# Loading q of two groups together in 1 KB pieces, and moving some loads and casts, in a chunked attention that feeds a squared-ReLU FFN

## The chip, the cores and the metric

The program runs on one core of one Trainium2 chip. The metric is the device time of one execution in microseconds (us); lower is better. A run's time is that of the whole execution; the span of a profile goes from its first to its last instruction and is a little shorter.

## The reference, cut to what matters

```
q, k, v: [8 batches, 8 heads, 576 tokens, 64] f32     # attention only inside chunks of 64 tokens
scores = q_c @ k_c^T / 8 ; attn = softmax(scores) ; a = attn @ v_c
x = a.transpose(0, 2, 1, 3).reshape(4608, 512)
h = relu(x @ w_in)          # w_in [512, 2048]
out = (h * h) @ w_out       # w_out [2048, 512], out f32
```

## The kernel before, in words

The 4608 tokens are cut into 18 **groups** of 256 tokens (four chunks of 64), and two groups make a **block** of 512 tokens; there are nine blocks, 0 to 8. Groups 0 to 13, 16 and 17 are "whole": their four chunks lie one after the other in one batch, and the two groups of a block are neighbours. Groups 14 and 15 (block 7) gather the ninth chunk of each batch.

A block's work is written in 32 to 46 **slots**: first the slots of its first matmul (`ffn_in`, or `ffn_in_unit` from block 2 on, which saves products by sums and differences; lines 607 and 494), then those of its second (`ffn_out`, line 664, seven products `n`, `m`, `n`, `m`, `n`, `m`, `n` that take 14 slots in the same way). A `yield` ends a slot. Between slots the loop at the end of the file (lines 873 to 958) inserts, by the table `plan`, the attention work of the **next** block and the casts and transposes of the block **after next**, and, in the slots listed in `go_slots`, one piece of the loads of the block after next. What is left of the loads is issued at the end of the block. All this fixes only the order of instructions on each engine. Each engine then runs its own list in that order and waits at semaphores. All loads, the DMA transposes and most stores are issued by SyncE (SP), so in one order.

The steps of a group `g`:

- `qk_pieces(g)` loads q and k in f32 (lines 106 and 120). For q, partition p of the tile holds two neighbouring tokens of all eight heads: 512 bytes lie together in HBM. For k (from group 4 on) a piece of 256 bytes is one token of one head. `v_pieces(g)` loads v for even and odd heads (lines 148 and 152), nine pieces for the two groups of a block, in 256-byte pieces.
- C (`cast_q`, `cast_k`; CQ and CK apart) turns them to bf16 in one tile `qkb`, on GpSimd for groups below 8, on ScalarE from 8 on (lines 334 and 341). For q it sorts by "plane": first all even tokens, then all odd ones.
- TD is the DMA transpose of `qkb` to `qkT` (line 352), from group 4 on; earlier groups are transposed by TensorE.
- SC (`scores`, line 375) multiplies a group's 32 pairs of 64x64 tiles into PSUM and takes the exponential on ScalarE (line 386), which also puts the planes' columns back in order of token.
- AV (`values`, line 403) multiplies by v and normalizes on VectorE (lines 410 and 411), giving `x`.
- XT transposes `x` to `xT`, which the next block's first matmul reads: by TensorE up to group 5, by DMA (line 424) from group 6 on.

In `ffn_out`, ScalarE copies the first `n` product out of PSUM (line 728), and the third product's running sum again (line 737); the fifth product adds into the same bank and so waits for that second copy. At the fixed slots of blocks 3 to 8 the casts of the block after next stand on ScalarE's list around these copies.

A few lines that the steps rest on:

```python
            elif j in UNITS:
                go_slots = range(35)
                if far and is_whole(far[0]):
                    go_slots = [*range(6), *range(13, 17), *range(23, 35)]
                slots.update({SC: (4, 4), AV: (8, 13), XT: (12, 17)})
                if j == 3 or not is_whole(nxt[0] if nxt else 0):
                    slots.update({SC: (8, 8), AV: (11, 16), XT: (14, 19)})
```

Here j is the running block, and each pair has the slots for the two groups of the next block. In block 2 the pairs are SC (8, 10), AV (12, 16), XT (15, 19), and the casts and TD of groups 8 and 9 have slots 23 to 28. In all blocks with a unit, slots 0 to 18 are the first matmul, slots 19 to 32 the second.

Of the kernel before, what the change touches and what calls it, by code (L numbers as in the profile page):

```python
# [17 lines left out]
def kernel(  # L18
# [9 lines left out]
    nc = tc.nc  # L28

    B, H, S, D = q.shape  # L30
# [13 lines left out]
    CH = GT // 4  # L44
# [3 lines left out]
    chunks = whole[:-2] + rest + whole[-2:]  # L48

    def is_whole(g):  # L50
        return chunks[g][0][0] == chunks[g][3][0]

    FIRST_DMA_T = 4
    FIRST_DMA_X = 6
    SQUARES_ON_ACT = (10, 14, 3)
# [44 lines left out]
    def qk_pieces(g):  # L100
        q_sb = in_pool.tile([128, 2, H, D], FP32, name="q_sb")
        k_sb = in_pool.tile([128, 2, H, D], FP32, name="k_sb")
        qk[g] = (q_sb, k_sb)

        def pairs(dst, src, p, m, b, s):
            return lambda: nc.sync.dma_start(
                out=dst.rearrange("p t h d -> p (t h d)")[p:p + m // 2, :].rearrange(
                    "p (h e) -> p h e", h=H),
                in_=src[b, :, s:s + m, :].rearrange("h (s i) d -> s h (i d)", i=2))

        if is_whole(g):
            yield pairs(q_sb, q, 0, GT, *chunks[g][0])
        else:
            for c in range(4):
                yield pairs(q_sb, q, c * CH // 2, CH, *chunks[g][c])
        if g < FIRST_DMA_T:
            yield pairs(k_sb, k, 0, GT, *chunks[g][0])
            return
        for t, p, m, b, s in runs(g):
            yield lambda t=t, p=p, m=m, b=b, s=s: nc.sync.dma_start(  # L120
                out=k_sb[p:p + m, t, :, :],
                in_=k[b, :, s:s + m, :].rearrange("h s d -> s h d"))
# [58 lines left out]
    state = {}  # L181
# [148 lines left out]
    def cast_q(g):  # L330
        qkb = att_pool.tile([128, 2, 2 * H * D], BF16, name="qkb", bufs=2)
        state["qkb", g] = qkb
        copy = nc.gpsimd.tensor_copy if g < 8 else nc.scalar.copy
        copy(
            out=qkb[:, 0].rearrange("p (i h d) -> p i h d", i=2, h=H),
            in_=qk[g][0].rearrange("p t h d -> p (t h d)").rearrange(
                "p (h i d) -> p i h d", h=H, i=2))

    def cast_k(g):
        copy = nc.gpsimd.tensor_copy if g < 8 else nc.scalar.copy  # L340
# [13 lines left out]
            in_=qkb.rearrange("p w c -> p (w c)"))  # L354

    def scores(g):
        qkT = state.pop(("qkT", g))
        by_plane = g >= FIRST_DMA_T

        def queries(a, t, hp, p):  # L360
            x = qkT[64 * a:64 * a + 64, 0]
            if by_plane:
                p0 = (2 * t + p) * CH // 2
                return x[:, :, hp, p0:p0 + CH // 2]
            return x[:, t, hp, p * 64:p * 64 + 64]

        ps = ps_att.tile([128, 1024], FP32, name="ps_att")
        for hp in range(n_hp):
            for t in range(2):
                for a in range(2):  # L370
                    for p in range(2):
                        c = p ^ a
                        cols = slice(p * 64, p * 64 + 64)
                        o0 = a * 512 + hp * 128 + t * 64
                        nc.tensor.matmul(  # L375
                            out=ps[64 * c:64 * c + 64, o0:o0 + 64],
                            lhsT=qkT[64 * a:64 * a + 64, 1, t, hp, cols],
                            rhs=queries(a, t, hp, p),
                            start=True, stop=True)
        e = att_pool.tile([128, 2, n_hp, 2, 64], BF16, name="e")  # L380
        state["e", g] = e
        e_out, s_in = e.rearrange("p a h t q -> p (a h t q)"), ps
        if by_plane:
            e_out = e.rearrange("p a h t (q i) -> p (a h t) q i", i=2)
            s_in = ps.rearrange("p (b i q) -> p b q i", i=2, q=CH // 2)
        nc.scalar.activation(out=e_out, in_=s_in, func=AF.Exp, scale=scale)  # L386

    def values(g, tiles=(0, 1)):
# [484 lines left out]
    for j, grps in enumerate(blocks):  # L873
        nxt = blocks[j + 1] if j + 1 < len(blocks) else []
        far = blocks[j + 2] if j + 2 < len(blocks) else []
        plan = {}

        def at(slot, f, g):
            plan.setdefault(slot, []).append((f, g))

        if j == 0:
            loads, go_slots = pieces(far), range(17)
            at(28, sum_quarters(b11_p_b21, b11, b21), None)
            for slot, f in ((24, TA), (27, SC), (29, AV), (31, XT)):
                at(slot, f, nxt[0])
            at(31, TQ, nxt[1])
            at(31, TK, nxt[1])
            at(31, sum_quarters(b11_m_b22, b11, b22, ALU.subtract), None)
            phases = [first_ffn_in, ffn_out_by_ft(0)]
        elif j == 1:  # L890
            loads, go_slots = itertools.chain(*map(qk_pieces, far)), range(26, 48)
            for slot, f in ((4, SC), (8, AV), (12, XT)):
                at(slot, f, grps[1])
            for i, g in enumerate(nxt):
                for slot, f in ((16 + 4 * i, C), (21 + 4 * i, TD), (36 + i, SC), (38 + 2 * i, AV),
                                (41 + 2 * i, XT)):
                    at(slot, f, g)
            for i, g in enumerate(far):
                at(36 + 4 * i, C, g)
                at(42 + 3 * i, TD, g)  # L900
            at(2, sum_quarters(b11_p_b12, b11, b12), None)
            at(12, sum_quarters(b12_p_b22, b12, b22), None)
            at(20, sum_quarters(b21_p_b22, b21, b22), None)
            phases = [ffn_in(1, [(0, 256, FT_ORDER), (256, 256, FT_ORDER)]), ffn_out(1)]
        else:
            loads, go_slots = pieces(far), range(32)
            slots = {SC: (4, 4), AV: (7, 11), XT: (10, 14), C: (18, 22), TD: (20, 24)}
            if j == 3:
                slots.update({SC: (8, 8), AV: (10, 14), XT: (13, 17)})
                go_slots = [*range(6), *range(13, 17), *range(20, 32)]  # L910
            if not is_whole(nxt[0] if nxt else 0):
                slots.update({SC: (6, 8), AV: (10, 14), XT: (12, 16)})
            if j == 2:
                loads = itertools.chain(*map(v_pieces, nxt), loads)
                slots = {SC: (8, 10), AV: (12, 15), XT: (15, 18), C: (20, 23), TD: (22, 25)}
                go_slots = [*range(16), *range(25, 36)]
            late_by = 0
            if j in UNITS:
                late_by = 3
            if j == 2:  # L920
                slots.update({AV: (12, 16), XT: (15, 19)})
                go_slots = [*range(16), *range(28, 39)]
            elif j in UNITS:
                go_slots = range(35)
                if far and is_whole(far[0]):
# [4 lines that stand above are left out]
            for f in (SC, AV, XT):  # L930
                for i, g in enumerate(nxt):
                    at(slots[f][i], f, g)
            if j > 2 and far and is_whole(far[0]):
                for slot, f, i in ((16, CQ, 0), (18, CK, 0), (18, TD, 0), (18, CQ, 1),
                                   (19, CK, 1), (19, TD, 1)):
                    at(slot + late_by, f, far[i])
            else:
                for f in (C, TD):
                    for i, g in enumerate(far):
                        at(slots[f][i] + late_by, f, g)  # L940
            phases = [ffn_in_unit(j) if j in UNITS else ffn_in(j, [(0, BT, FT_ORDER)]),
                      ffn_out(j)]
        slot = 0
        for phase in phases:
            for _ in phase:
                if slot in go_slots:
                    for f in loads:
                        f()
                        break
                for f, g in plan.get(slot, []):  # L950
                    f(g)
                while late and (slot >= LATE_STORES.get(j, 99) or (j, slot) == (2, 9)):
                    late.pop(0)()
                slot += 1
        assert all(x < slot for x in plan), (j, slot, sorted(plan))
        go(loads)
        while late and j > 1:
            late.pop(0)()
# [30 lines left out]
```

## Time and profile before

| | |
|---|---|
| time before, median of 3 runs | 279.32 us (279.13 to 279.36) |
| the profiled execution's own time | 282.07 us |
| its span | 280.3 us |
| TensorE (PE) busy | 269.5 us, 96% |
| VectorE (DVE) busy | 205.2 us, 73% |
| ScalarE (ACT) busy | 155.7 us, 56% |
| GpSimd (POOL) busy | 95.4 us, 34% |
| DMA queue of SP, share of 16 engines' time | 84.8% |
| q loads of 512 KB | 16, 6.4 us from issue to landing (median) |
| q-k DMA transposes | 14, 4.8 us |
| x DMA transposes | 12, 3.6 us |

Views are named by what they are: the page's table of engines and its rows of 40 slices (each digit is the busy share of 1/40 of the span in tenths; PEclk is the granted TensorE clock), the list of waits of one engine, and the timeline of one engine, where a row reads: start in us, duration in us, engine, line, operation, output<-inputs, count, and in brackets the idle time before it and what ended it. "SPq" rows are issues by SyncE: their duration is that of issuing, not of the transfer. "Landing" is when a transfer's last part has arrived.

### The profile page before, as it was taken

The page shows a single profiled execution, that of the slowest core. Times are in us where ns is not written, and L with a number is a line of the kernel's source. Part 1 is how long each engine was busy: PE and PEld are TensorE (multiplying, and loading weights), DVE is VectorE, ACT ScalarE, POOL GpSimd, SP SyncE. Part 2 cuts the span into 40 slices and gives each one's busy share as a digit, 9 for nine tenths or more (in the row PEclk, how much of TensorE's full clock was granted, in tenths as well). Part 3 has the DMA queues.
Part 4 walks back from the last instruction along what each step waited for, and adds up shares of the span by engine and source line. Part 5 has one row for each costly group of instructions (what it writes and reads, how often), then busy time and mean ns, then how long its engine had stood idle before and what let it go on. Part 6 is the DMA issues. An engine that isn't in the chain of part 4 may idle for free.

```text
span 280.3 us, 7376 instructions
## 1 busy us (share of the span) xinstructions
PE 269.5 (96%) x3047; PEld 186.2 (66%) x3047; DVE 205.2 (73%) x313; ACT 155.7 (56%) x262; POOL 95.4 (34%) x110
## 2 busy tenths in 40 slices
PE   6987999999999999899999999999999999999995
PEld 4642445788785678457855785578558855885684
DVE  0542704899888798689868795979589949786794
ACT  1544713787426765579265927583779185507710
POOL 2036868351043810172017301720190019003403
PEclk9997999999999999999999999999999999999999
DMA  6999999989999879999999999897699992204004
GB/s 230 234 337 336 303 347 243 310 223 214 181 223 170 208 234 205 246 272 235 204 212 267 219 186 294 190 153 165 152 295 224 180 274 39 40 22 130 0 0 152
DMA packets 141313, 57.11 MB, mean 204 GB/s; under 512 B 110368, under 2 KB 135200, under 8 KB 141280
## 3 DMA queue, kind: packets, MB, share of 16 engines
q1 hardware_dynamic: 140544, 54.67, 84.8%
q0 software_dynamic: 592, 1.84, 1.7%
q8 instruction: 24, 0.39, 0.6%
q10 hardware_dynamic: 144, 0.13, 0.1%
q14 instruction: 9, 0.07, 0.1%
HBM read 36.70 MB, written 9.44 MB: 165 GB/s over the span
## 4 chain that ended last, share of the span: by engine, by line
PE 50%; DVE 0%; issue 0%
PE ps_ffn L664 24%; PE ps_ffn L607 19%; PE ps_ffn L494 6%; PE ps_att L403 1%; PE ps_att L375 1%; DVE o_sb L769 0%
## 5 line engine op out<-in xcount | busy, mean ns | idle before, releaser
L607 PE MATMUL ps_ffn<-xT,w_in_bf 128*128 128x512 bf16 (+1 forms) x528 | 112.7, 357 | 2.9 <-POOL w_in_bf L166 2.0
L620 POOL TENSOR_TENSOR gT<-rl 128x512 bf16<-128x512 f32 x40 | 45.5, 1152 | 121.5 <-ACT rl L571 118.3
L607 PEld LDWEIGHTS <-w_in_bf 128*128 128x128 bf16 x528 | 50.9, 99 | 40.8 <-POOL w_in_bf L166 2.5
L664 PEld LDWEIGHTS <-w_st 128*128 128x128 bf16 x640 | 62.2, 98 | 7.7 <-issue 0.4
L571 ACT ACTIVATE rl<-ps_ffn 128x512 f32<-128x512 f32 x84 | 50.0, 596 | 30.4 <-PE ps_ffn L607 30.2
L620 DVE TENSOR_TENSOR w_st<-gT 128x2048 bf16<-128x2048 bf16 x40 | 47.4, 1219 | 6.0 <-ACT gT L574 5.9
L664 PE MATMUL ps_ffn<-w_out_bf,w_st 128*128 128x256 bf16 x384 | 45.1, 273 | 0.0
L620 DVE TENSOR_TENSOR gT<-rl 128x512 bf16<-128x512 f32 x30 | 20.7, 691 | 21.1 <-ACT rl L571 20.7
L664 PE MATMUL ps_ffn<-w_sum,w_st 128*128 128x256 bf16 x256 | 29.6, 273 | 0.2 <-ACT n L737 0.2
L664 PEld LDWEIGHTS <-gT 128*128 128x128 bf16 x256 | 24.7, 98 | 5.0 <-ACT gT L574 0.5
L602 DVE TENSOR_TENSOR gT<-rl 128x256 bf16<-128x256 bf16 (+1 forms) x41 | 18.5, 491 | 10.2 <-ACT rl L598 9.8
L598 ACT ACTIVATE rl<-ps_ffn 128x256 bf16<-128x256 f32 (+1 forms) x48 | 20.3, 455 | 9.6 <-PE ps_ffn L607 8.9
L511 DVE SCALAR_TENSOR_TENSOR gT<-rl 128x512 bf16<-128x512 f32 x21 | 23.2, 1103 | 0.4
L411 DVE TENSOR_TENSOR x<-ps_att,rec 128x512 bf16<-128x512 f32 x32 | 22.1, 691 | 1.1
L771 ACT COPY o_sb<-ps_ffn 128x512 f32<-128x512 f32 x7 | 4.1, 585 | 30.4 <-PE ps_ffn L664 30.4
L386 ACT ACTIVATE e<-ps_att 128x1024 bf16<-128x1024 f32 x16 | 15.8, 1023 | 5.4 <-PE ps_att L375 5.4
L494 PEld LDWEIGHTS <-w_dif 128*128 128x128 bf16 x140 | 13.1, 98 | 7.5
L664 PE MATMUL ps_ffn<-w_out_bf,gT 128*128 128x256 bf16 x128 | 15.6, 273 | 0.0
L664 PE MATMUL ps_ffn<-w_sum,gT 128*128 128x256 bf16 x128 | 15.3, 273 | 0.0
L166 POOL CAST w_in_bf<-w_st 128x1024 bf16<-128x1024 f32 (+1 forms) x9 | 8.7, 969 | 19.0 <-DMA w_st<-in_moe_w_in_dram 19.0
L620 DVE TENSOR_TENSOR w_st<-xT 128x1024 bf16<-128x1024 bf16 (+1 forms) x21 | 12.5, 652 | 2.8 <-DMA xT<-x 2.0
L781 PE MATMUL ps_ffn<-w_out_bf,gT 128*128 128x512 bf16 x64 | 14.5, 380 | 0.0
(82 smaller groups left out, 294.2 us busy)
## 6 DMA issues: line engine op xcount, KB each, us to landing
q_sb<-in_q_dram SPq DMA_DIRECT2D x16, 512.0 KB, 6.4
k_sb<-in_k_dram SPq DMA_DIRECT2D x24, 256.0 KB, 6.0
out_dram<-o_sb SPq DMA_DIRECT2D x12, 512.0 KB, 4.3
w_st<-in_moe_w_in_dram SPq DMA_DIRECT2D x8, 512.0 KB, 8.6
w_st<-in_moe_w_out_dram SPq DMA_DIRECT2D x8, 512.0 KB, 6.0
ve_sb<-in_v_dram SPq DMA_DIRECT2D x28, 128.0 KB, 3.2
vo_sb<-in_v_dram SPq DMA_DIRECT2D x21, 128.0 KB, 3.1
k_sb<-in_k_dram SPq DMA_DIRECT2D x4, 512.0 KB, 6.8
```

What stands on the lines that cost most here:

```text
L166: nc.gpsimd.tensor_copy(out=w_in_bf[:, :, i * 256 + c:i * 256 + c + n], in_=st[:, :, c:c + n])
L386: nc.scalar.activation(out=e_out, in_=s_in, func=AF.Exp, scale=scale)
L411: nc.vector.tensor_tensor(out=x[:, t].rearrange("p h a d -> p a h d"), in0=o[:, :, :, 0:D], in1=rec.to_broadcast([128, 2, n_hp, D]), op=AL ...
L494: nc.tensor.matmul(out=out[:, 256 * f:256 * f + 256], lhsT=a[:, d, 128 * f:128 * f + 128], rhs=b[:, :, d, :], start=(first and f == 0 and ...
L511: later.append(lambda: nc.vector.scalar_tensor_tensor(out=place_of(i, jj), in0=both(x), scalar=0.0, in1=both(x), op0=ALU.max, op1=ALU.mult))
L571: nc.scalar.activation(out=rl, in_=h, func=AF.Relu)
L598: nc.scalar.activation(out=rl[:, 0:n], in_=h[:, 0:n], func=AF.Relu)
L602: nc.vector.tensor_tensor(out=gT[:, ft, c:c + n], in0=rl[:, 0:n], in1=rl[:, 0:n], op=ALU.mult)
L607: nc.tensor.matmul(out=h[:, 0:n], lhsT=w_in_bf[:, dt, ft * 128:(ft + 1) * 128], rhs=xT[:, c // 128:(c + n) // 128, dt, :], start=(dt == 0) ...
L620: engine.tensor_tensor(out=out, in0=in0, in1=in1, op=op)
L664: nc.tensor.matmul(out=outs[t], lhsT=a[:, i, t * 128:(t + 1) * 128], rhs=b[:, i, :], start=(first and i == 0 and (last or t == 0)), stop=( ...
L781: nc.tensor.matmul(out=o_ps[tt], lhsT=gT[:, ft, tt * 128:(tt + 1) * 128], rhs=w_out_bf[:, ft, :], start=(ft == 0), stop=(ft == n_ft - 1))
```

## The change

- **q in pairs.** For whole groups from 6 on (6 to 13, 16, 17) the two loads of a block no longer bring one group's 256 tokens of eight heads each, but the block's 512 tokens of four heads each; a partition holds four neighbouring tokens, and 1 KB lies together in HBM. The number of loads and their bytes stay. The cast sorts into four planes instead of two, the exponential undoes four, and the scores of either group read the queries out of both groups' `qkT`, as four runs of 16 columns instead of two runs of 32.
- **V of group 5** is loaded in block 1 from slot 26 on, behind TD of groups 4 and 5 (slots 21 and 25), instead of in block 0.
- **q and k of group 9** are loaded in block 2 in slots 20 to 22, behind XT of groups 6 and 7 (slots 15 and 19), instead of in slots 12 to 14; all V pieces of groups 8 and 9 follow from slot 28 on (one of them stood in slot 15).
- **Casts of group 11** in block 3 stand in slots 25 and 26 instead of 21 and 22, and its TD in 26 instead of 22.
- XT of group 3 in block 1 stands in slot 13 instead of 12.

```diff
+    def is_joint(g):
+        return g >= FIRST_JOINT and is_whole(g)
+
+    FIRST_JOINT = 6
...
-        if is_whole(g):
+        if is_joint(g):
+            b, s0 = chunks[g - g % 2][0]
+            h0 = H // 2 * (g % 2)
+            yield lambda: nc.sync.dma_start(
+                out=q_sb.rearrange("p t h d -> p (t h d)").rearrange("p (h e) -> p h e", h=H // 2),
+                in_=q[b, h0:h0 + H // 2, s0:s0 + BT, :].rearrange("h (s i) d -> s h (i d)", i=4))
+        elif is_whole(g):
             yield pairs(q_sb, q, 0, GT, *chunks[g][0])
...
+        n = 4 if is_joint(g) else 2
         copy(
-            out=qkb[:, 0].rearrange("p (i h d) -> p i h d", i=2, h=H),
+            out=qkb[:, 0].rearrange("p (i h d) -> p i h d", i=n, d=D),
             in_=qk[g][0].rearrange("p t h d -> p (t h d)").rearrange(
-                "p (h i d) -> p i h d", h=H, i=2))
+                "p (h i d) -> p i h d", i=n, d=D))
...
-        qkT = state.pop(("qkT", g))
+        qkT = state["qkT", g]
         by_plane = g >= FIRST_DMA_T
+        n_planes = 4 if is_joint(g) else 2
 
         def queries(a, t, hp, p):
+            if is_joint(g):
+                x = state["qkT", g - g % 2 + hp // 2][64 * a:64 * a + 64, 0].rearrange(
+                    "c t h q -> c (t h) q").rearrange("c (i h) q -> c i h q", i=4)
+                p0 = (4 * (g % 2) + 2 * t + p) * CH // 4
+                return x[:, :, hp % 2, p0:p0 + CH // 4]
...
-            e_out = e.rearrange("p a h t (q i) -> p (a h t) q i", i=2)
-            s_in = ps.rearrange("p (b i q) -> p b q i", i=2, q=CH // 2)
+            e_out = e.rearrange("p a h t (q i) -> p (a h t) q i", i=n_planes)
+            s_in = ps.rearrange("p (b i q) -> p b q i", i=n_planes, q=CH // n_planes)
...
         if j == 0:
-            loads, go_slots = pieces(far), range(17)
+            loads = itertools.chain(*map(qk_pieces, far), v_pieces(far[0]))
+            go_slots = range(17)
...
         elif j == 1:
-            loads, go_slots = itertools.chain(*map(qk_pieces, far)), range(26, 48)
-            for slot, f in ((4, SC), (8, AV), (12, XT)):
+            loads = itertools.chain(v_pieces(nxt[1]), *map(qk_pieces, far))
+            go_slots = range(26, 48)
+            for slot, f in ((4, SC), (8, AV), (13, XT)):
...
             if j == 2:
                 slots.update({AV: (12, 16), XT: (15, 19)})
-                go_slots = [*range(16), *range(28, 39)]
+                go_slots = [*range(12), *range(20, 23), *range(28, 39)]
...
             if j > 2 and far and is_whole(far[0]):
-                for slot, f, i in ((16, CQ, 0), (18, CK, 0), (18, TD, 0), (18, CQ, 1),
-                                   (19, CK, 1), (19, TD, 1)):
+                q1, k1 = (22, 23) if j == 3 else (18, 19)
+                for slot, f, i in ((16, CQ, 0), (18, CK, 0), (18, TD, 0), (q1, CQ, 1),
+                                   (k1, CK, 1), (k1, TD, 1)):
                     at(slot + late_by, f, far[i])
```

(`late_by` is 3 in every block with a unit.)

## The prediction

> **What bounds the kernel now.** I read the page first, then the waits of PE, then the timelines around each of them. A measurement of this kernel can tell about 0.2% (0.56 us) from no change.
>
> ```profile
> PE 269.5 (96%) x3047; PEld 186.2 (66%) x3047; DVE 205.2 (73%) x313; ACT 155.7 (56%) x262; POOL 95.4 (34%) x110
> ...
> PEclk9997999999999999999999999999999999999999
> DMA  6999999989999879999999999897699992204004
> ```
>
> PE is the bound, at 96%. The DMA engines are nearly as full for the first 200 us, so a transfer that PE needs can come late only because others lie ahead of it. PE's list of waits says where that happens:
>
> ```profile
> PE ps_ffn L607 <- POOL w_in_bf L166: 2.0, 1, 2.0
> ...
> PE ps_ffn L607 <- DMA xT<-x: 0.9, 1, 0.9
> ...
> PE ps_att L375 <- DMA qkT<-qkb: 0.5, 1, 0.5
> ...
> PE ps_ffn L664 <- ACT n L737: 0.2, 1, 0.2
> ```
>
> The other waits lie in the first 23 us or are PE's own attention chain (0.38 us at 59.90). PE's timeline gives places for the three that remain: block 1's scores of group 5, the start of block 3, and the fifth product of block 3.
>
> ```profile
> 74.89 0.45 PE L375 MATMUL ps_att<-qkT 64*64 64x64 bf16 x32 [0.51 <-DMA qkT<-qkb]
> ...
> 113.10 2.76 PE L607 MATMUL ps_ffn<-xT,w_in_bf 128*128 128x512 bf16 x12 [0.90 <-DMA xT<-x]
> ...
> 135.87 1.36 PE L664 MATMUL ps_ffn<-w_sum,w_st 128*128 128x256 bf16 x11 [0.25 <-ACT n L737]
> ```
>
> 0.51 + 0.90 + 0.25 = 1.66 us is all that loads, transposes and casts cost PE after the start; from 135.87 on the chain that ended last is matmuls alone. So 1.66 us is also the most that this change can win in the profiled execution.
>
> **V of group 5 behind the transposes: the wait of 0.51.** SP's timeline:
>
> ```profile
> 64.52 1.06 SPq L148 DMA_DIRECT2D ve_sb<-in_v_dram  x2
> 65.62 1.16 SPq L152 DMA_DIRECT2D vo_sb<-in_v_dram  x2
> 66.95 5.60 SPq L352 DMA_TRANSPOSE qkT<-qkb  x2
> ```
>
> The two first rows are V of group 5, four issues in 2.43 us (64.52 to 66.95). Without them the transposes of 4 and 5 issue that much earlier; the cast of group 5's k, which the second needs, is done at 65.29 (64.19 + 1.10), so at most 0.8 us of it is held back. The wait of 0.51 goes. The V pieces then issue at about 70 to 72 and land by 75 (the two rows above landed 2.8 to 3.1 us after issue); AV of group 5 is at 78.6. The loads of groups 6 and 7 behind them stay where they were: what is ahead of them is the same in sum.
>
> **q in pairs.** 512 KB in 512-byte pieces against 1 KB pieces: GpSimd's casts of w_in (1 KB pieces, 512 KB each) start as their loads land, at 23.23, 24.70, 26.16, 27.51 and 28.86, so 1.35 to 1.47 us apart. For q, ScalarE's timeline in block 2 does the same service:
>
> ```profile
> 105.06 1.05 ACT L341 CAST qkb<-k_sb 128x1024 bf16<-128x1024 f32 x1 [1.77 <-DMA k_sb<-in_k_dram]
> 106.01 0.58 ACT L737 COPY n<-ps_ffn 128x512 f32<-128x512 f32 x1
> 107.03 1.05 ACT L334 CAST qkb<-q_sb 128x1024 bf16<-128x1024 f32 x1 [0.45 <-DMA q_sb<-in_q_dram]
> 109.47 1.04 ACT L341 CAST qkb<-k_sb 128x1024 bf16<-128x1024 f32 x1 [1.39 <-DMA k_sb<-in_k_dram]
> ```
>
> Each cast starts as its load lands: 107.03 - 105.06 = 1.97 us for one q. So a joint q saves about 0.5 us of the queue, 1.0 us a block of some 27.5 us. By itself this moves PE by nothing; it is slack for the transposes. The Trainium skill speaks against it: "DMA: Bandwidth & Descriptors", section Specifications, puts line rate at 512 bytes and more, so 1 KB would gain nothing. These rows differ (1.97 against 1.35 to 1.47), and I go by them; by the page the three waits would still go, but the slack would not come, and the last transpose of block 6 (below) would cost 0.65.
>
> Its price elsewhere: the casts read other strides, but row L334 (strided, 1.05) and row L341 (contiguous, 1.04) cost the same. The exponential with four planes is in the trace already: the first block's (L286) takes 1023 ns, those with two planes (L386) 1006 to 1032. Four runs of 16 columns in a matmul's moving operand are not in the trace. One run of 64 (block 1, 46.56) and two runs of 32 (block 2, 72.96) both take 0.45 us for 32 recorded matmuls, so I take zero; the far bound is that they double, 0.64 us for each of five pairs of groups, 3.2 us; a gain is excluded, since no step is left out.
>
> Either group's scores now wait for both transposes. From block 3 on both stand in the same slot, so at most 0.3 us is lost of any margin. In block 2 slots 8 and 10 differ: scores of group 6 start at 90.96, and group 7's transpose lands at 85.85 + 4.3 = 90.2. It issued when group 7's k cast ended (84.55 + 1.27); with two shorter q and the group-5 transposes gone earlier it should land 1 to 3 us sooner, PE arrives 0.5 sooner: no wait.
>
> **q and k of group 9 behind XT: the wait of 0.90.** SP issued these ahead of the two x transposes of block 2:
>
> ```profile
> 99.31 3.82 SPq L106 DMA_DIRECT2D q_sb<-in_q_dram  x1
> 103.17 1.78 SPq L120 DMA_DIRECT2D k_sb<-in_k_dram  x2
> 105.00 1.60 SPq L148 DMA_DIRECT2D ve_sb<-in_v_dram  x1
> 106.70 4.27 SPq L424 DMA_TRANSPOSE xT<-x  x2
> ```
>
> x of group 7 is finished at 101.37 (100.68 + 0.69), yet its transpose issues at 108.37 and lands 4.7 later, at 113.05. With the four issues behind it, XT issues at about 101.5 and lands near 105, PE reading it at 112.2: the wait goes with 7 us to spare. SP now waits for x with q and k of group 9 queued behind it: they issue at about 103 instead of 99.31 to 104.95. Their service is 1.45 for q and 2.44 (109.47 - 107.03) for k, so k lands at 108 to 109, before as now about 109.4, and ScalarE's cast is no later. The V pieces of group 8 land by 119 as now; AV needs them at 122.2.
>
> **Casts of group 11 behind the copy: the wait of 0.25.** Line 737's copy stood behind two casts, one of which waited 0.64 for k:
>
> ```profile
> 132.59 1.05 ACT L334 CAST qkb<-q_sb 128x1024 bf16<-128x1024 f32 x1
> 134.28 1.05 ACT L341 CAST qkb<-k_sb 128x1024 bf16<-128x1024 f32 x1 [0.64 <-DMA k_sb<-in_k_dram]
> 135.24 0.58 ACT L737 COPY n<-ps_ffn 128x512 f32<-128x512 f32 x1
> ```
>
> With the copy first, PE's wait goes. The casts follow it (two of 1.05) and end about where the second ended. The transpose of group 11 pays: SP now issues four V pieces (2.3 us, 0.57 each) ahead of it. Before, it issued at 139.14, landed 4.5 later at 143.6, and the scores of block 4 stood at 145.09.
>
> **The sum.** 282.07 - 1.66 = 280.41 for the profiled execution. That one was 2.75 above the median: it ran 21 to 28 us at a clock of 0.76 (7 x 0.24 = 1.7) and lost 2.0 to w_in, both before any of this. If the median's runs have neither, PE comes 0.94 sooner than the whole difference tells, so the DMA waits there are larger and 2.6 is won; if only the 2.0 is missing and the queue is 2.75 ahead, the waits are 0.75 smaller and 0.9 is won. I take 1.66 off the median: 279.32 - 1.66 = 277.66, say 277.7.
>
> **Rivals.** *A new wait takes part of it back* (0.18): block 4's scores, or block 7's, whose last transpose lands at 221.77 + 4.8 = 226.6 against scores at 227.60; PE 1.66 sooner is at 225.94, which 1.0 of shorter q just covers (without it 0.65 is lost). Price 0.3 to 1.2: 278.0 to 278.9. *Slower* (0.11), one mechanism: the transpose of group 11 behind its later cast and four V pieces. If SP's queue in block 3 is no earlier than now, it issues at 139.14 + 2.3 = 141.4, lands at 145.9, and PE, at 145.09 - 1.66 = 143.4, waits 2.5: 280.2. It decides from an issue later than 138.9. Against it: q8 to q11 give 2.0 us of queue, and slices 14 and 15 of the DMA row (91 to 105 us) are only 8 and 7 tenths full, to be filled by issues that come sooner. *No change* (0.09): the 1 KB pieces and moves free the queue, but the next block waits by the same amount, as would be if the queue's total set the pace; its 9s speak for it, PE's lack of any wait after 136 against it: 279.3. Clear gain without such a wait: 0.62.
>
> **How the numbers follow.** Faster 0.62 + 0.18 = 0.80, same 0.09, slower 0.11. The range runs from 276.7 (2.6 won) to 279.0 (most of a new wait) and leaves out the no-change and slower cases.
>
> **What would show it.** Right: no DMA wait over 0.15 in PE's list after 60 us; XT of group 7 landing before 107; line 737 in block 3 ahead of group 11's casts; 269.5 of PE busy kept. Wrong: the row L375 at 120, 143 or 226 behind qkT, or 64 of its matmuls longer than 0.71 us.

## The result and the profile after

| | before | changed |
|---|---|---|
| median of 20 executions | 279.45 us (278.69 to 281.06) | 282.64 us (280.19 to 287.05) |
| ratio | | 1.0097, 95% interval 1.0078 to 1.0117 |
| the profiled execution, its span | 282.07, 280.3 | 280.5, 278.7 |

The change makes the kernel about 1% slower, 3.2 us by the medians (the ratio is a little smaller, since it leaves out executions more than 1.5% above the fastest of their kernel). The two traces alone would say the opposite: before was profiled in an execution slower than any of the 20, the changed kernel in one of its quickest. So the waits have to be compared, not the spans. The first three of PE's waits in the changed kernel:

```profile
PE ps_att L392 <- DMA qkT<-qkb: 2.7, 1, 2.7
PE ps_ffn L337 <- POOL ident L76: 1.7, 1, 1.7
PE ps_ffn L624 <- POOL w_in_bf L176: 0.9, 2, 0.7
```

(Lines are shifted: L392 is the score matmul that was L375, L624 was L607, L363 is the q-k transpose that was L352, L158 and L162 load v.) The waits of 0.51, 0.90 and 0.25 that the prediction set out to remove are gone, all three: after 23 us the list has only its first line and one of 0.2 us for `xT` in block 1. In their place stands one of 2.66 us, in the middle of group 10's scores in block 4. PE's timeline:

```profile
140.67 0.32 PE L392 MATMUL ps_att<-qkT 64*64 64x64 bf16 x16
143.65 0.57 PE L392 MATMUL ps_att<-qkT 64*64 64x64 bf16 x48 [2.66 <-DMA qkT<-qkb]
```

The first half of the head pairs reads group 10's `qkT` and runs; the second half lies in group 11's, since q comes in pairs now, and has to wait. SP's timeline says why that transpose is late:

```profile
133.27 1.97 SPq L363 DMA_TRANSPOSE qkT<-qkb  x1
135.29 0.57 SPq L162 DMA_DIRECT2D vo_sb<-in_v_dram  x1
135.91 1.11 SPq L158 DMA_DIRECT2D ve_sb<-in_v_dram  x2
137.06 0.51 SPq L162 DMA_DIRECT2D vo_sb<-in_v_dram  x1
137.67 2.45 SPq L363 DMA_TRANSPOSE qkT<-qkb  x1
```

Group 11's k cast on ScalarE ended at 132.4 (131.33 + 1.05), before SP had even issued group 10's transpose:

```profile
131.33 1.05 ACT L352 CAST qkb<-k_sb 128x1024 bf16<-128x1024 f32 x1
```

SP could have issued group 11's at 135.29; it first issued the four V pieces that now stand in slots 23 to 26, and the transpose went at 137.67 and landed 5.9 later, at 143.6.

A second trace of the changed kernel (284.43 us; run `e8_after_again` below) shows another wait, of which the first trace had 0.09 us:

```profile
PE ps_att L392 <- DMA qkT<-qkb: 2.2, 1, 2.2
PE ps_att L420 <- DMA vo_sb<-in_v_dram: 2.0, 1, 2.0
```

L420 are the value matmuls (before: L403), here group 8's in block 3. The first row below is PE's; the others are SP's, where their last V piece stands behind a store:

```profile
122.87 0.19 PE L420 MATMUL ps_att<-vo_sb,e 64*64 64x65 bf16 x1 [2.05 <-DMA vo_sb<-in_v_dram]
...
105.97 5.66 SPq L363 DMA_TRANSPOSE qkT<-qkb  x1
...
112.98 1.70 SPq L363 DMA_TRANSPOSE qkT<-qkb  x1
114.73 0.58 SPq L158 DMA_DIRECT2D ve_sb<-in_v_dram  x1
115.36 1.26 SPq L162 DMA_DIRECT2D vo_sb<-in_v_dram  x2
116.72 0.45 SPq L732 DMA_DIRECT2D out_dram<-o_sb  x1
117.27 0.42 SPq L162 DMA_DIRECT2D vo_sb<-in_v_dram  x1
```

The piece issued at 117.27 landed 5.6 later, at 122.8, where the other four pieces, ahead of the store, took 2.7 to 3.1; the four V pieces next behind it took 4.7 to 5.6. Before, one V piece of group 8 was issued in slot 15, so all five were ahead of that store. The change took that slot away and with it moved the fifth piece behind 512 KB of output.

### The profile page after: what moved, and what is told of

It is laid out like the page before. It is cut to its first block, busy times and chain, and to the rows that moved or that the text cites. A ratio compares the mean times of both kernels' runs of the same rounds, so it can differ in the third digit from the quotient of the medians.

```text
span 278.7 us, 7377 instructions
## 1 busy us (share of the span) xinstructions
PE 267.1 (96%) x3047; PEld 185.0 (66%) x3047; DVE 205.6 (74%) x313; ACT 155.5 (56%) x262; POOL 95.0 (34%) x110
## 4 chain that ended last, share of the span: by engine, by line
PE 84%; DMA 6%; SPq 4%; DVE 2%; issue 1%; POOL 0%; ACT 0%; DVEq 0%
PE ps_ffn L624 33%; PE ps_ffn L681 33%; PE ps_ffn L511 8%; PE ps_ffn L798 5%; SPq L247 3%; DMA w_st<-in_moe_w_in_dram 3%; DMA qkT<-qkb 2%; PE ps_att L420 2%; PE ps_att L392 1%; DMA vo_sb<-in_v_dram 1%; DVE w_st L637 1%; PE ps_att L447 1%; SPq L238 1%; PE ps_att L201 1%; DVE x L428 1%
## 5 line engine op out<-in xcount | busy, mean ns | idle before, releaser
L624 PE MATMUL ps_ffn<-xT,w_in_bf 128*128 128x512 bf16 (+1 forms) x528 | 111.4, 353 | 1.1 <-POOL w_in_bf L176 0.9
L624 PEld LDWEIGHTS <-w_in_bf 128*128 128x128 bf16 x528 | 50.4, 98 | 38.2 <-POOL w_in_bf L176 2.4
L403 ACT ACTIVATE e<-ps_att 128x1024 bf16<-128x1024 f32 x16 | 15.8, 1021 | 7.4 <-PE ps_att L392 7.4
L591 ACT ACTIVATE gT<-rl 128x512 bf16<-128x512 f32 x21 | 13.2, 630 | 0.7
```

Source lines behind the costliest of these rows:

```text
L591: nc.scalar.activation(out=gT[:, ft], in_=rl, func=AF.Square)
L624: nc.tensor.matmul(out=h[:, 0:n], lhsT=w_in_bf[:, dt, ft * 128:(ft + 1) * 128], rhs=xT[:, c // 128:(c + n) // 128, dt, :], start=(dt == 0) ...
```

## The experiments

Each ratio is against the kernel before, run beside it on the same chip; its median there was 278.92 us for `e1` to `e4` and 279.59 for `e9` to `e12`, of 33 executions each. `e5` to `e8` are one execution each; beside them the kernel before ran once, in 282.06 us, so its slower executions are not only the profiled one.

**The casts and the transpose of group 11 back in slots 21 and 22** (`e1_casts_back`).

```diff
-                q1, k1 = (22, 23) if j == 3 else (18, 19)
+                q1, k1 = 18, 19
```

> The changed kernel with the casts of group 11 and its transpose back in slots 21 and 22 of block 3, ahead of line 754's copy and of the four V pieces. Theory A (the transpose of group 11 stands behind four V pieces on SP, lands at 143.6 and makes block 4's scores wait 2.66 us): the transpose issues near 135, lands by 140.5, the 2.66 goes, a wait of 0.25 to 0.5 for the copy comes back in block 3; time 278.0 to 279.0, below the kernel before. Theory B (the queue's total work sets the pace, so that the wait only moves): a wait of over 1.5 us for a transfer stands elsewhere in blocks 3 to 5; time 281 or more.

279.72 us, ratio 1.0032 (0.9998 to 1.0065). No wait at block 4's scores; the copy's wait is back at 0.58; group 8's V costs 0.39:

```profile
118.96 0.19 PE L420 MATMUL ps_att<-vo_sb,e 64*64 64x65 bf16 x1 [0.39 <-DMA vo_sb<-in_v_dram]
...
132.62 3.65 PE L681 MATMUL ps_ffn<-w_sum,w_st 128*128 128x256 bf16 x32 [0.58 <-ACT n L754]
```

Theory A's order of things holds and B's does not, but the time is above A's 278 to 279.

**Block 3's V pieces behind that transpose, the casts left late** (`e2_v_last`).

```diff
-                    go_slots = [*range(6), *range(13, 17), *range(23, 35)]
+                    go_slots = [*range(6), *range(13, 17), *range(27 if j == 3 else 23, 35)]
```

> The changed kernel with the last five V pieces of block 3 issued from slot 27 on, behind the transpose of group 11 (slot 26), the casts staying behind the copy. Theory A: SP issues the transpose at about 135.3 in place of 137.7, it lands near 140, block 4's scores (141.0) wait under 0.3 us, no copy wait in block 3; time 277.5 to 278.5. Theory C (the later casts themselves, not the V pieces, hold the transpose): the wait stays above 1.5 us and the time above 280.5. Theory B: as in the run with the casts back, 281 or more.

279.36 us, ratio 0.9995 (0.9967 to 1.0023). SP now issues both transposes one after the other and the V pieces after them:

```profile
131.73 1.26 SPq L441 DMA_TRANSPOSE xT<-x  x1
133.09 4.69 SPq L363 DMA_TRANSPOSE qkT<-qkb  x2
137.83 0.57 SPq L162 DMA_DIRECT2D vo_sb<-in_v_dram  x1
```

The scores wait for nothing. So it is the V pieces, not the later casts (theory C), that held the transpose. The profiled execution took 277.69, as A expects, but the median is no better than before, and the executions fall into two groups, 277.3 to 278.2 and 279.1 to 280.9. That was still open.

**Only the move of the casts, on the kernel before** (`e3_cast_only`).

```diff
-                for slot, f, i in ((16, CQ, 0), (18, CK, 0), (18, TD, 0), (18, CQ, 1),
-                                   (19, CK, 1), (19, TD, 1)):
+                q1, k1 = (22, 23) if j == 3 else (18, 19)
+                for slot, f, i in ((16, CQ, 0), (18, CK, 0), (18, TD, 0), (q1, CQ, 1),
+                                   (k1, CK, 1), (k1, TD, 1)):
```

> The kernel before with only the move of group 11's casts and transpose to slots 25 and 26 of block 3; q stays in 512-byte pieces and no load is moved. Theory A: the transpose again issues some 2.3 us later, behind four V pieces, and group 11's scores in block 4 wait 0.7 to 2.7 us, against 0.25 won at the copy; time 279.8 to 282.0. Theory D (the pairing of q, through which group 10's scores too need group 11's transpose, is what costs): no wait above 0.4 us at block 4's scores; time 279.0 to 279.5.

282.04 us, ratio 1.0081 (1.0049 to 1.0114). This one move makes nearly the whole loss, without pairs of q and without any other move, and the time is at the top of theory A's 279.8 to 282.0; theory D falls. SP issued group 11's transpose at 138.69, behind four V pieces from 136.12 on. Here the wait cuts group 10's scores from group 11's, and the granted clock falls right after it (columns of the second view: stretch, its length, busy time of PE, PEld, DVE, ACT and POOL, granted clock, DMA share, GB/s):

```profile
144.53 0.45 PE L375 MATMUL ps_att<-qkT 64*64 64x64 bf16 x32 [2.71 <-DMA qkT<-qkb]
```

```profile
138.00:145.00 7.00, 4.29 (x83) 2.33 (x82) 2.15 (x4) 3.96 (x7) 1.04 (x1) 1.00 1.16 206
145.00:149.00 4.00, 4.00 (x16) 1.93 (x16) 1.38 (x2) 2.21 (x3) 0.00 (x0) 0.57 1.04 319
149.00:156.00 7.00, 7.00 (x101) 4.04 (x100) 6.15 (x13) 3.22 (x6) 5.92 (x5) 1.00 1.51 234
```

A clock of 0.57 over 4 us is 1.7 us of PE work lost in this execution on top of the 2.7.

**The wait filled with matmuls** (`e4_filled`).

```diff
         for hp in range(n_hp):
+            if g == 10 and hp == 2:
+                for _ in range(25):
+                    nc.tensor.matmul(
+                        out=ps[:, 256:512], lhsT=ident, rhs=ident_f32.bitcast(BF16),
+                        start=True, stop=True)
```

> The changed kernel with 25 matmuls of 256 columns (some 2.7 us) put between the first and the second half of group 10's scores, into columns that the second half then overwrites; PE works where it idled. Theory H (after the idle 2.66 us the granted clock falls to half for 3.4 us in most executions, which is why the median lies 2 us above the profiled one): no wait at block 4's scores, the clock stays at 1.00 there; time 280.2 to 281.0, little spread. Theory W (the clock has no part in it; the wait alone is longer in most executions): time 282.3 to 283.0 as without the filling, or more, since the matmuls are added to a wait that is longer than they are.

282.17 us, ratio 1.0102 (1.0065 to 1.014). The clock part came as H expects: the mean clock was 0.995 or less in 3 of 10 executions, against 17 of 20 of the changed kernel, and in the trace it stays at 1.00 there, with 0.18 left of the wait (this trace's own stretch of half clock starts at 12.7 us). The time did not: 282.2 is above H's 280.2 to 281.0, and just under W's 282.3 to 283.0. The filling did not touch the wait for group 8's V, found only later (`e8_after_again`). The 25 matmuls themselves took 2.90 us of PE, a little more than the 2.66 of the wait in the changed kernel's first trace. So theory H's account of the median is not borne out, and what the clock alone costs is not separated by this run.

**Further traces** of the kernel before, of the kernel of `e2_v_last` and of the changed kernel, without an edit.

> The kernel before once more, for a second trace. If the three waits of 0.51, 0.90 and 0.25 are its usual state, they stand here too (sum 1.2 to 2.6 us) in an execution of about 279; if they belong to the one profile with the 2.0 us wait for w_in and the clock cut, their sum is under 0.8 us.

279.22 us. The wait for x at block 3 is missing here, those for the transposes of groups 4 and 5 sum to 0.4, and the copy's is larger, 0.56 instead of 0.25. The sum lies between the two expectations: 0.6 + 0.4 = 1.0 us is what there was to win in this execution, which lies near the median, not 1.66:

```profile
PE ps_ffn L664 <- ACT n L737: 0.6, 1, 0.6
PE ps_att L375 <- DMA qkT<-qkb: 0.4, 2, 0.3
```

Block 3's two q-k transposes and block 4's scores stood here, the second transpose issuing at 135.6 and landing 4.9 later:

```profile
133.76 4.45 SPq L352 DMA_TRANSPOSE qkT<-qkb  x2
...
142.16 0.71 PE L375 MATMUL ps_att<-qkT 64*64 64x64 bf16 x64
```

> The kernel with the V pieces last once more. Its first trace (277.7) has no wait over 0.2 us after 25 us, yet half of its executions take 279 to 281. If those lose their time before 30 us (start, weights, clock), an execution of that kind shows over 2 us more of waits and slow clock there and none later; if they lose it to a transfer later, a wait over 1 us stands at a scores, values or x row after 60 us.

> The same kernel and question as the run before it; two looks, since each execution may be of either kind.

278.16 and 278.43 us: both of the quicker kind, with no wait over 0.25 us after 25 us. No trace shows the slower kind.

> The changed kernel once more. Expected: the wait of block 4's scores for group 11's transpose again, 2.0 to 5 us; where the execution takes over 282, either the wait is longer than 2.66 or the granted clock is 0.5 for 3.4 us right after it.

284.43 us, with both waits shown above, 2.24 and 2.05 us, and no clock cut (mean 1.0). Neither of the two things expected of an execution above 282 is there; the second wait, which was not expected, stands in their place and leads to the next theory.

**Both late transfers repaired** (`e9_both`): the edit of `e2_v_last`, and one V piece of group 8 more ahead of block 2's transposes, so that all five come before the store.

```diff
-                go_slots = [*range(12), *range(20, 23), *range(28, 39)]
+                go_slots = [*range(12), *range(20, 24), *range(28, 39)]
```

> The kernel with the V pieces of block 3 last, and one V piece of group 8 more issued in block 2 ahead of the transposes (slots 20 to 23 in place of 20 to 22), so that all five pieces of group 8 stand ahead of the first late store. Theory A2 (two transfers came late in the changed kernel: group 11's transpose, and in some executions group 8's last V piece, which stands behind a store): neither wait is left over 0.2 us, the upper half of the times (279 to 281) goes; median 0.8 to 1.4 us below that of before. Theory P (the rest of the spread is the chip's start and clock): median as with the first repair alone, within 0.6 us of before, still in two groups.

277.78 us (276.44 to 278.83), ratio 0.9924 (0.9899 to 0.9949): below both kernels, and by more than A2's 0.8 to 1.4 us; no execution took over 279. The end of PE's list follows, without its last line, a 0.2 put down to issue. Only that one and the 0.2 for `xT` lie after 23 us:

```profile
PE ps_ffn L624 <- POOL w_in_bf L176: 0.4, 1, 0.4
PE ps_att L309 <- DVE x L317: 0.3, 1, 0.3
PE ps_ffn L624 <- ACT xT L452: 0.2, 1, 0.2
```

**Only the second repair** (`e10_v8_only`): this edit without that of `e2_v_last`.

> The changed kernel with only the second repair: five V pieces of group 8 ahead of the late store, while block 3's V pieces stay ahead of group 11's transpose. Theory A2: the wait of block 4's scores stays at 2.0 to 3.0 us, no wait at the values of group 8; median 0.5 to 1.5 us above before, that is 1 to 2 us below the changed kernel. Theory P: as the changed kernel, 2.5 to 3.5 us above before.

281.93 us, ratio 1.0065 (1.0034 to 1.0097); the scores wait 3.19 us, the values of group 8 not at all. But the median is 2.3 us above before, outside A2's 0.5 to 1.5 and just under P's 2.5 to 3.5, and its interval overlaps that of the changed kernel (1.0078 to 1.0117): by itself the second repair is not shown to gain. With three other kernels this makes a square (each ratio against the kernel before beside it, on more than one chip):

| ratio to before | group 8's fifth V piece behind the store | ahead of it |
|---|---|---|
| block 3's V ahead of group 11's transpose | 1.0097 (the change) | 1.0065 |
| behind it | 0.9995 | 0.9924 |

The order of the V pieces against the transpose is worth 1.0 to 1.4%. The fifth V piece is worth 0.7% once that order is right, where the intervals are apart (0.9967 to 1.0023, 0.9899 to 0.9949); the 0.3% without it is within the noise. That this piece made the upper group of `e2_v_last` follows from the group's going, not from a trace of it.

**q in 512-byte pieces, all else repaired** (`e11_q_512`).

```diff
-    FIRST_JOINT = 6
+    FIRST_JOINT = 99
```

> Both repairs, but q in 512-byte pieces again, each group with its own tokens. If the 1 KB pieces save 0.4 to 0.9 us of the queue each, as the landings say, the margins shrink by 0.8 to 1.8 us a block: group 11's transpose or group 8's V lands so late that a wait of 0.3 to 1.5 us returns; median 0.3 to 1.5 us above the run with both repairs. If the pieces bring nothing on the queue, the two medians agree within 0.3 us.

278.17 us, ratio 0.9949 (0.9923 to 0.9975), 0.4 us above the run with both repairs; the intervals overlap. The trace has no wait over 0.23 us after 25 us, so the wait that was expected to return did not. What 1 KB pieces add to the time once the orders are right stays undecided. What they save on the queue can be added up from the packets in the traces: a q load in 512-byte pieces took 1.94 to 1.98 us of the 16 DMA engines (both traces of before, and this run), a joint one 1.73 to 1.78 (both traces of the changed kernel, `e9_both`, `e12_q_only`; packets that start between 60 and 215 us). That is 0.2 us a load.

**q in pairs alone, on the kernel before** (`e12_q_only`): the new functions with the old tables of slots.

> The kernel before with q in pairs and 1 KB pieces alone, no load or cast moved. By the prediction this moves PE by nothing by itself, but shortens the waits on the queue: median 0 to 0.8 us below before; the wait for x at block 3 and that for group 5's transpose stay or shrink, the copy wait of 0.25 to 0.56 stays. If the pairing costs (four runs of 16 columns, or group 10's scores waiting for group 11's transpose), 0.3 us or more above before, with longer score matmuls or a wait at scores.

278.74 us, ratio 0.9971 (0.9943 to 0.9999). A small gain, 0.85 us by the medians: in its one trace the waits for x, for the transpose and for the copy are all below 0.15 us. The copy's wait was expected to stay. The score matmuls with four runs of 16 columns take 186 to 215 ns in the changed kernel's trace, with a median of 193, as before (186 to 214, 193); the pairing costs nothing there.

## Why the prediction was wrong

- **What bounds the kernel:** right. PE is the bound, and what is to be won or lost is its few waits for transfers.
- **The three waits:** right in kind. All are gone in the changed kernel. That a move is the reason is shown for the copy alone, whose wait returns when the casts go back (0.58 in `e1_casts_back`). For the other two it stays open: with q in pairs and no move at all (`e12_q_only`) none of the three is over 0.15 either. Their size was taken from one execution: 1.66 us there, 1.0 in the second trace. The kernel with both repairs is 0.76% below before, 1.8 us by the medians. That this is near the 1.66 forecast for the change is partly luck, since it is more than the 1.0 that the second trace had to give.
- **The step that failed** is the relief for group 11's transpose: "q8 to q11 give 2.0 us of queue", 0.5 for each q in 1 KB pieces. The prediction saw the mechanism ("SP now issues four V pieces (2.3 us, 0.57 each) ahead of it"), priced its wait at 2.5 and gave it 0.11 as the slower rival; the wait measured 2.66 and 2.24, and 3.19 in `e10_v8_only`. It was set aside because q8 to q11 and the slack slices were to bring the queue forward by 2.0 us and more. The 0.5 came from comparing q with w_in's loads; the packets give 0.2 a load, 0.8 for four. And the queue came forward by less than that: SP issued group 10's transpose at 133.27, against 133.76 in the usual execution of before, `e5_before_again` (0.5 us sooner), while PE reached the scores at 140.67 instead of 142.16 (1.5 us sooner). The prediction itself had put group 9's k at 108 to 109 behind x (before: 106.14 in the usual execution; after: 109.33), and its transpose waits for that k's cast: SP issued it at 110.48 after, 110.36 before. So at that point the queue was no earlier at all. `e3_cast_only`, with 512-byte pieces and the loads of group 9 where they were, waits about as long, 2.71.
- **The point from which it decides** was given as an issue later than 138.9, on the clock of an execution in which PE was 3 us late. In the trace after, the scores were due at 141.0 and the landing took 5.9, so the point was 135.1; the issue came at 137.67. Taken as a distance inside one trace it would have shown: before, the transpose landed 1.5 us ahead of the scores in the profiled execution (143.6 against 145.09) and 1.7 in the usual one (140.5 against 142.16), both less than the four V pieces' 2.3.
- **Group 8's V** was passed over with "land by 119 as now; AV needs them at 122.2". That counted the V pieces and not the store between them, and it took the due time from the same late execution: at 118.1 in the trace after. What the lost slot 15 does to the fifth piece's place on SP's queue was not followed.
- **No price for what a wait does to the clock.** The trace of before had it in front: 2.0 us of wait for w_in, then a clock of 0.76 over 21 to 28 us. The prediction treated both as accidents of that execution. So even its slower rival, 280.2, is 2.4 us below the measured median. The three executions of the changed kernel with a mean clock of 0.999 or more took 280.4 to 280.8 us, the twelve at 0.993 and 0.994 had a median of 282.5, the five at 0.988 one of 284.5. That points to the clock, but it is not shown: `e3_cast_only` has no such steps, `e4_filled` is no faster with fewer cuts, and `e8_after_again` took 284.43 without a cut.
- **The 1 KB rule.** The Trainium skill's "DMA: Bandwidth & Descriptors", section Specifications, puts line rate at 512 bytes. The prediction went by the rows instead. The measurement lies between the two: packets of 1 KB saved 0.2 us a load, not nothing and not 0.5, and `e12_q_only` is 0.3% below before, with an interval that ends at 0.9999.

## What to carry to other kernels

When a step is moved on one engine, look up what its follower is moved past on the queue that issues it: here two casts went four slots later on ScalarE at no cost, and their DMA transpose fell behind four loads on SP. Judge a margin as a distance between landing and need inside one trace, preferably of two executions, and not against absolute times from an execution that was itself delayed. Where several transfers are just in time, look for the next one after a repair: with the transpose's order right the kernel was level with before (0.9995), and the gain came with the second repair (0.9924).

## What the runs showed of the hardware

- **A wait of 2 to 3 us on PE can be followed by half clock.** By the clock records of the traces, each one with a mean clock below 0.995 has a stretch of half clock in its first 150 us, 3.4 us long (6.8 in `e11_q_512`). It lies 1.0 us behind the 2.71 us wait in `e3_cast_only` and 1.1 us behind the 2.0 us wait for w_in in the first trace of before, but at 12.2 to 12.9 us in the others, `e10_v8_only` with its 3.19 us wait among them; the two traces of the changed kernel (2.66; 2.24 and 2.05) have none. So of four traces with the wait at block 4's scores, one shows the cut there. Counts of executions agree with a link but do not say where the cut lay: with that wait the mean clock was 0.995 or less in 17 of 20 (the change), 11 of 12 (`e10_v8_only`) and 9 of 12 (`e3_cast_only`); without it in 15 of 66 (before), 3 of 12 (`e2_v_last`), 3 of 10 (`e9_both`), 3 of 10 (`e4_filled`), 2 of 12 (`e12_q_only`), 5 of 12 (`e11_q_512`) and 7 of 12 (`e1_casts_back`). The Trainium skill, "TensorE: Matmul & The Clock Gate", section "Part 1: The HAM clock gate (the "warmup" mystery)", describes a free-running window of 3413 ns whose activity sets the clock, with half clock after at least one idle window. The trace of `e3_cast_only` agrees with a cut of that length (0.57 over 4 us); the wait ahead of it, 2.71 us, was shorter than a window.
- **A transpose's issue can hold SP for long.** Group 8's issue took 5.4 to 5.7 us on SP where it stood right behind q and k of group 9 (the two traces of the changed kernel), 3.8 and 3.9 with a V piece between (`e9_both`, `e10_v8_only`), 1.8 in the kernel before; everything behind it, group 8's V among it, waited. That a limit on outstanding transfers does this was not tried.
